# Chunk-selected attention followed by a gated feed-forward: constants in small parts, the first batch staged in half slots, a new order of work

## The chip, the cores and the metric

The kernel runs on one NeuronCore of a Trainium2 chip. The metric is device time in microseconds of one launch, measured over several runs; beside it stands one execution recorded by the hardware profiler. Engines are named as the profile names them: PE is TensorE's matmuls and PEld its weight loads, DVE is VectorE, ACT is ScalarE, POOL is GpSimd, and SP is SyncE, which in this kernel issues the DMAs. SPq is SyncE's queue.

## What is computed

Four batches of eight heads, 768 positions of 64 numbers each, in float32. The keys of a head are cut into 24 chunks of 32. For every query an upper bound of its product with any key of a chunk is formed from the chunk's smallest and largest key values, and only the six chunks with the highest bounds are attended to, causally. The result of all heads is the input of a feed-forward stage of width 2048 with a gate.

```python
k_min, k_max = np.min(k_chunks, axis=3), np.max(k_chunks, axis=3)
ub = np.sum(np.maximum(q * k_min, q * k_max), axis=-1)      # one bound for each query and chunk
ub = np.where(causal, ub, -1e9)
top_chunks = np.argsort(ub, axis=-1)[..., -6:]
scores = scale * np.matmul(q, k.transpose(0, 1, 3, 2))
scores = np.where(selected_chunk & (query_pos >= key_pos), scores, -1e9)
attn = softmax(scores)
x = np.matmul(attn, v)          # heads side by side: 3072 tokens x 512
h = x @ w_in                    # 512 -> 2048
g = h * np.clip(h + 3.0, 0.0, 6.0) / 6.0
out = g @ w_out                 # 2048 -> 512, float32
```

## The kernel before

**One list sets everything.** The work is cut into about 1,100 small steps. A text, `ORDER` (lines 34 to 108), lists them by short names; a loop at the end looks each name up in a table (line 620) and issues its instructions. Every engine works through its instructions in the order of that list, and so does SyncE through its DMAs; an instruction starts when its engine has come to it and what it reads or overwrites is ready or free. Nothing else orders the work: the place of a step in the list decides what stands before it on its engine. A letter at the end of a name (a, b, c, x, y) is the PSUM place that the step writes.

**Prologue.** `PRP` (line 259) lets GpSimd make the causal biases of the bounds (BIASM) and a chunk selector, built in a tile called E0 that lies inside XT; `PRI` (line 256) makes the identity that TensorE's transposes need, on GpSimd; `PRL` (line 273) casts the identity to bfloat16 and clears EM on VectorE; `PRD` (line 248) clears, on VectorE, a tiny tile, the operand of the warm-up matmuls (WARM, also inside XT) and constant columns of other tiles; `EG` (line 277) spreads the chunk selector into EM; `PRA` (line 245) runs one dummy exponential on ScalarE; `Z` (line 280) issues warm-up matmuls whose result is not used; `bd` (line 356), later, makes the biases of the other batches on GpSimd.

**Batch 0** is worked pair by pair: four pairs of heads, each in a first and a second half of 384 positions. `LK`, `LQ` and `LV` (line 363) load a half of one head's keys, queries or values, 98 KB each, from SyncE. `KT` and `QT` (line 375) turn a half, three 128x128 transposes on TensorE into PSUM. From there ScalarE casts it to bfloat16 (`KB`, `QB`), VectorE takes the largest and smallest key of each chunk (`MX`, `MN`, line 389), and the positive and negative parts of the queries are written (`RP` on ScalarE, `RN` on VectorE, `RA` on ScalarE; lines 399 to 409). `UH` forms the bounds on TensorE, `UB` adds the bias on VectorE, `TH` turns them, `T8` and `SE` find the six best chunks on VectorE, and `LH` and `MT` bring the choice back as a mask operand. `S` computes scores with the mask added in PSUM, `ex` exponentiates them on ScalarE (line 497), `af` cuts the causal triangle on GpSimd (line 501), `VC` casts a half of V on GpSimd (line 371), `A` and `B` multiply with V, and `na` and `nb` normalise on VectorE (line 534).

The inputs of batch 0 are staged in a float32 tile, STAGE, of six slots of 768 columns: K and Q of pairs 0 to 2 fill them, and pair 3 reuses those of pair 0 (lines 149 and 150). V has two slots (VS), pairs 0 and 2 in one, pairs 1 and 3 in the other.

**Batches 1 to 3** are worked four heads at once, a quad, of which there are two per batch, numbered 2 to 7. `lk` and `lq` load 192 KB for each head from SyncE into a third of STAGE (line 218), `lv` loads V for one pair; `kd` and `qd` are block transposes on VectorE (line 226), `mx` and `mn` reductions there (line 298), `kb` and `qb` casts on ScalarE, `rp` the positive part; `ud` forms the bounds, `us`, `tr`, `tm`, `se` and `tb` select on VectorE, and `mv` gathers on GpSimd; `SQ` computes scores for the quad.

**Feed-forward**: groups of 384 tokens, two per batch, numbered 0 to 7. `X` and `xe` turn the attention's result by TensorE for groups 0 to 2, `xt` (line 545) by DMA from SyncE for the rest. `wl` loads a quarter of a weight matrix, 1 MB (line 237), `wc` casts it on GpSimd (line 241): 0 to 3 are `w_in`, 4 to 7 `w_out`, through two buffers. A hidden step `H` is eight matmuls (line 562), with its gate on ScalarE (`hu`, line 571) and VectorE (`gt`, line 576). An output step `O` is four matmuls of 512 columns (line 597), four of them fill one PSUM bank, which `ot` unloads on ScalarE and `st` stores from SyncE.

## Time and profile before

| | |
|---|---|
| median of 3 runs | 284.9 us (283.8 to 286.69) |
| the profiled execution | 283.9 us, its span 282.2 us |
| PE busy | 261.6 us, 93% of the span |
| DVE busy | 182.9 us, 65% |
| ACT busy | 181.2 us, 64% |
| POOL busy | 104.6 us, 37% |
| read from HBM | 27.26 MB, written 6.29 MB |
| loads of batch 0's keys and queries | 32 of 96 KB, 2.4 and 2.5 us from issue to landing (medians) |

The span runs from the first to the last profiled instruction of the program; the profiled execution's own time contains it and 1.7 us around it. Busy time of PE comes from matmuls whose ends are modelled, so a busy PE is not a PE at its peak. A row of the timeline gives a start, a duration, engine, line of the kernel, operation, output and inputs and a count of merged instructions; behind it, in brackets, how long the engine stood idle before it and what ended that. A row of waits gives the waiting instruction, what it waited for, the total in microseconds, how often, and the longest.

### The profile page before, as it was taken

The page shows a single profiled execution, that of the slowest core. Times are in us where ns is not written, and L with a number is a line of the kernel's source. Part 1 is how long each engine was busy: PE and PEld are TensorE (multiplying, and loading weights), DVE is VectorE, ACT ScalarE, POOL GpSimd, SP SyncE. Part 2 cuts the span into 40 slices and gives each one's busy share as a digit, 9 for nine tenths or more (in the row PEclk, how much of TensorE's full clock was granted, in tenths as well). Part 3 has the DMA queues.
Part 4 walks back from the last instruction along what each step waited for, and adds up shares of the span by engine and source line. Part 5 has one row for each costly group of instructions (what it writes and reads, how often), then busy time and mean ns, then how long its engine had stood idle before and what let it go on. Part 6 is the DMA issues. An engine that isn't in the chain of part 4 may idle for free.

```text
span 282.2 us, 8568 instructions
## 1 busy us (share of the span) xinstructions
PE 261.6 (93%) x3549; PEld 153.7 (54%) x3549; DVE 182.9 (65%) x448; ACT 181.2 (64%) x251; POOL 104.6 (37%) x246
## 2 busy tenths in 40 slices
PE   0987998799999999999999999999999999999994
PEld 0555676566545456665555456665555555555561
DVE  1577798589997969999985538673783313622610
ACT  2377898347688648983567799878758752623621
POOL 6410296472860577540071454450481430000000
PEclk9999999999999999999999999999999999999999
DMA  5788449798999696494066544196000220221111
GB/s 128 162 192 178 163 96 324 155 324 251 247 242 205 173 202 151 92 222 65 2 144 132 126 92 110 41 200 118 6 0 14 103 56 2 74 95 38 74 55 58
DMA packets 91479, 36.08 MB, mean 128 GB/s; under 512 B 84144, under 2 KB 84400, under 8 KB 91440
## 3 DMA queue, kind: packets, MB, share of 16 engines
q1 hardware_dynamic: 91440, 35.53, 54.7%
q8 instruction: 28, 0.46, 0.7%
q14 instruction: 11, 0.09, 0.1%
HBM read 27.26 MB, written 6.29 MB: 119 GB/s over the span
## 4 chain that ended last, share of the span: by engine, by line
PE 63%; POOL 9%; DMA 8%; DVE 5%; issue 4%; ACT 3%; SPq 1%; POOLq 0%; DVEq 0%; ACTq 0%
PE PSx L604 12%; PE PSy L604 9%; PE PBa L566 8%; PE PBc L566 7%; PE PBb L566 7%; POOL MQ L353 4%; DMA WS<-in_moe_w_in_dram 3%; PE PSy L522 3%; DMA VS<-in_v_dram 2%; DMA STAGE<-in_q_dram 2%; PE PBb L604 2%; POOL WIN L243 2%; PE PBc L489 2%; PE PBb L489 2%; PE PBa L489 2%
## 5 line engine op out<-in xcount | busy, mean ns | idle before, releaser
L566 PEld LDWEIGHTS <-WIN 128*128 128x128 bf16 x512 | 49.0, 98 | 35.2 <-issue 1.5
L604 PEld LDWEIGHTS <-GT 128*128 128x128 bf16 x368 | 32.9, 98 | 38.9 <-issue 3.5
L506 POOL TENSOR_SCALAR_AFFINE_SELECT PT<-PT 128x256 bf16<-128x256 bf16 x78 | 30.4, 414 | 57.3 <-ACT PT L499 57.0
L604 PE MATMUL PSx<-WOUT,GT 128*128 128x512 bf16 x176 | 43.4, 380 | 0.6 <-POOL WOUT L243 0.6
L353 POOL COPY MQ<-MTM 32x144 bf16<-32x144 bf16 x96 | 29.4, 306 | 29.3 <-DVE MTM L347 25.0
L604 PE MATMUL PSy<-WOUT,GT 128*128 128x512 bf16 x144 | 35.1, 380 | 0.0
L499 ACT ACTIVATE PT<-PBc 128x1024 bf16<-128x1024 f32 (+2 forms) x29 | 25.7, 887 | 14.5 <-PE PBc L493 9.7
L566 PE MATMUL PBa<-XT,WIN 128*128 128x384 bf16 x184 | 33.7, 326 | 0.0
L574 ACT ACTIVATE U<-PBa 128x768 bf16<-128x768 f32 x23 | 18.7, 812 | 22.9 <-PE PBa L566 22.1
L566 PE MATMUL PBb<-XT,WIN 128*128 128x384 bf16 x160 | 29.3, 326 | 1.7 <-POOL WIN L243 1.3
L566 PE MATMUL PBc<-XT,WIN 128*128 128x384 bf16 x168 | 30.8, 326 | 0.0
L577 DVE SCALAR_TENSOR_TENSOR GT<-U,PBa 128x768 bf16<-128x768 bf16 x23 | 21.8, 947 | 13.1 <-ACT U L574 13.1
L577 DVE SCALAR_TENSOR_TENSOR GT<-U,PBc 128x768 bf16<-128x768 bf16 x21 | 20.0, 951 | 12.9 <-ACT U L574 12.8
L229 DVE STREAM_TRANSPOSE STAGE<-STAGE 128x768 f32<-128x768 f32 x24 | 23.0, 965 | 6.3 <-DMA STAGE<-in_q_dram 3.6
L499 ACT ACTIVATE PT<-PBb 128x1024 bf16<-128x1024 f32 (+2 forms) x25 | 23.5, 940 | 3.6 <-PE PBc L493 1.8
L574 ACT ACTIVATE U<-PBb 128x768 bf16<-128x768 f32 x20 | 16.2, 812 | 14.4 <-PE PBb L566 13.9
L499 ACT ACTIVATE PT<-PBa 128x1024 bf16<-128x1024 f32 (+2 forms) x24 | 22.7, 948 | 2.9 <-PE PBa L493 2.7
L577 DVE SCALAR_TENSOR_TENSOR GT<-U,PBb 128x768 bf16<-128x768 bf16 x20 | 19.0, 948 | 8.2 <-ACT U L574 7.9
L574 ACT ACTIVATE U<-PBc 128x768 bf16<-128x768 f32 x21 | 17.0, 810 | 9.4 <-PE PBc L566 8.4
L301 DVE TENSOR_REDUCE KMA<-STAGE 128x24 f32<-128x768 f32 x24 | 22.1, 940 | 0.1
L522 PEld LDWEIGHTS <-PT 128*128 128x128 bf16 x546 | 19.1, 97 | 3.9 <-issue 1.3
L489 PEld LDWEIGHTS <-KBA 32*128 32x128 bf16 x480 | 9.3, 92 | 16.5 <-issue 13.8
(191 smaller groups left out, 462.4 us busy)
## 6 DMA issues: line engine op xcount, KB each, us to landing
out_dram<-OT SPq DMA_DIRECT2D x23, 256.0 KB, 2.4
STAGE<-in_k_dram SPq DMA_DIRECT2D x24, 192.0 KB, 5.3
STAGE<-in_q_dram SPq DMA_DIRECT2D x24, 192.0 KB, 5.2
VS<-in_v_dram SPq DMA_DIRECT2D x12, 384.0 KB, 5.6
WS<-in_moe_w_in_dram SPq DMA_DIRECT2D x4, 1024.0 KB, 7.1
WS<-in_moe_w_out_dram SPq DMA_DIRECT2D x4, 1024.0 KB, 6.1
STAGE<-in_k_dram SPq DMA_DIRECT2D x16, 96.0 KB, 2.4
STAGE<-in_q_dram SPq DMA_DIRECT2D x16, 96.0 KB, 2.5
```

The source lines that it names most:

```text
L229: nc.vector.transpose(out=T, in_=T)
L243: nc.gpsimd.tensor_copy(WIN[:, :, 512 * c:512 * (c + 1)] if n < 4 else WOUT[:, 4 * c:4 * c + 4, :], WS[n % 2][:])
L301: nc.vector.tensor_reduce(out=dst, in_=staged("k", n)[:, h], axis=AX.X, op=(A.max, A.min)[w])
L353: nc.gpsimd.tensor_copy(MQ[n % 2][CH * g:CH * (g + 1), w * part:w * (part + 1)], MT4[n % 2][CH * part:CH * (part + 1), w * g:w * (g + 1)])
L489: nc.tensor.matmul(PSB[both[g // 2]][:, g % 2, at:at + w], lhsT=K[rows, x, j * P:(j + 1) * P], rhs=Q[rows, x, q0:q0 + w], start=(x == 0), ...
L499: nc.scalar.activation(pt(i, u)[:, :, 0:n], PSB[slot["S", i, u]][:, :, 0:n], ACT.Exp, scale=float(scale))
L506: nc.gpsimd.affine_select(out=T[:, :, lo:lo + P], in_=T[:, :, lo:lo + P], pattern=[[0, 2], [1, P]], compare_op=A.is_ge, fill=0.0, base=0, ...
L522: nc.tensor.matmul(O[:, e, t, :], lhsT=pt(i, u)[:, e, lo:lo + P], rhs=VB[i % 4][:, j, e, :], start=(j == 0), stop=(j == qb))
L566: nc.tensor.matmul(PSB[c][:, ff, 0:GRP], lhsT=WIN[:, kt, (2 * f + ff) * P:(2 * f + ff + 1) * P], rhs=XT[g % 3][:, kt, :], start=(kt == 0), ...
L574: nc.scalar.activation(slot["R", g, f][:], PSB[slot["H", g, f]][:, :, 0:GRP], ACT.Relu, bias=3.0)
L577: nc.vector.scalar_tensor_tensor(out=GT[g % 2][:, 2 * f:2 * f + 2, :], in0=slot["R", g, f][:], scalar=6.0, in1=PSB[slot["H", g, f]][:, :, ...
L604: nc.tensor.matmul(PSS[c], lhsT=GT[g % 2][:, f, t * P:(t + 1) * P], rhs=WOUT[:, f, :], start=(f == 0), stop=(f == FT - 1))
```

## The change

Three things are edited, and the list is written anew.

*Constants.* The five prologue steps become ten: `PW` clears the warm-up operand, `PT` the tiny tile, `PO` fills the constant columns, `PI` makes the identity, `PR` casts it, `PB` makes the biases of the bounds, `PF` fills E0 (on VectorE, before on GpSimd), `PC` cuts it on GpSimd, `PZ` clears EM and, new there, the bias tile of the other batches in one memset on VectorE, which `bd` cleared in four on GpSimd; `PA` is the dummy exponential. In the new list VectorE begins with `PW` and GpSimd with `PI`. There are six warm-up matmuls where there were five.

*Staging of batch 0.* STAGE is addressed by half slots: twelve of 384 columns, so that K and Q of all four pairs' first halves and of pairs 0 and 1's second halves have places of their own, and the second halves of pairs 2 and 3 reuse those of the first halves of pairs 0 and 1. V has one half slot for each pair; its second half follows into the same place after the first has been cast.

*Queues.* Six Q half loads (`AQ`: both heads of the first halves of pairs 0, 1 and 2) are issued from ScalarE's queue; three stand in the list ahead of the dummy exponential and three behind it. The other ten Q loads, all K and all V loads stay with SyncE.

*Order.* All other steps keep their instructions, with two exceptions in number: the negative part of second halves is written by VectorE for pairs 1 and 3 (`RN`) and by ScalarE for pairs 0 and 2 (`RA`), where ScalarE wrote all four. The first two lines of the new list, and pieces further on that the text below speaks of:

```diff
 ORDER = """
...
+PW AQ.2.0.1 LK.0.0.0 PT PI PO LK.0.1.1 AQ.0.0.1 PR Z.y.6 PZ PF PB LK.0.0.1 KT.0.0.b PC AQ.0.0.0 MX.0.0 EG.2 LK.1.0.1
+MN.0.0 EG.0 LK.1.0.0 PA EG.1 QT.0.0.y AQ.1.0.1 EG.3 AQ.1.0.0 LK.0.1.0 AQ.2.0.0 RP.0.0 RN.0.0 KT.1.0.a MN.1.0 MX.1.0
+KB.0.0 QB.0.0 QT.1.0.x KT.0.1.y RP.1.0 KB.1.0 RN.1.0 UH.0.0.c UH.1.0.b QB.1.0 MN.0.1 KB.0.1 LQ.0.1.1 UB.1.0 UB.0.0
...
+na.2 S.2.3.c ex.2.3 T8.3.1 LV.0.1.1 SE.3.1 wl.0 S.2.5.a X.0.1.x xe.0.1 S.2.2.b ex.2.2 LH.3.1.y MT.3.1 wc.0 af.0.2
+wl.1 kd.2.0 mx.2.0 H.0.1.c hu.0.1 ex.2.5 gt.0.1 mn.2.0 af.1.2 af.0.3 LV.0.1.0 VC.0.1 B.0.0.x H.0.0.b hu.0.0 gt.0.0
...
+qb.3.0 wl.6 wc.6 se.2.0 ud.3.b.a tb.2.0 mv.2.1 mv.2.0 us.3.1 tr.3.1 H.1.7.c hu.1.7 lv.5 wl.7 us.3.0 lk.4 H.1.4.a
+wc.7 hu.1.4 vc.5 gt.1.7 tm.3.1 O.0.2.2.x SQ.2.5.c.b lq.4 ex.5.5 gt.1.4 qb.3.1 O.0.0.2.y SQ.2.4.b.a ex.4.5 af.4.5
...
+gt.2.6 B.7.0.y qb.5.1 B.7.1.y B.6.1.x kb.5.1 nb.6 mv.4.1 SQ.4.4.b.c ex.9.4 H.2.7.a hu.2.7 nb.7 O.2.2.0.x lv.11 xt.3
+ex.8.4 gt.2.7 H.2.4.c hu.2.4 gt.2.4 SQ.4.5.a.b ex.9.5 tr.5.0 ex.8.5 tm.5.0 lk.7 tm.5.1 O.2.0.0.y O.2.0.1.y kb.5.0
+vc.8 SQ.4.0.a.c ex.8.0 se.5.0 tb.5.0 H.3.5.b ex.9.0 mv.5.0 hu.3.5 af.9.5 O.2.0.2.y O.2.0.3.y H.3.1.a af.8.5 gt.3.5
...
+hu.7.6 gt.7.6 H.7.7.a ot.6.1 hu.7.7 gt.7.7 H.7.2.b hu.7.2 gt.7.2 H.7.0.c hu.7.0 st.6.0 H.7.5.a hu.7.5 gt.7.0 H.7.4.b
+hu.7.4 gt.7.4 O.7.0.0.x O.7.0.1.x O.7.1.0.c O.7.1.1.c st.6.1 gt.7.5 O.7.0.2.x O.7.1.2.c O.7.1.3.c ot.7.1 O.7.0.3.x
...
-    KS = [STAGE[:, 2 * i % 6].rearrange("p (j e d) -> p j e d", e=2, d=D) for i in range(NPAIR)]
-    QS = [STAGE[:, (2 * i + 1) % 6].rearrange("p (j e d) -> p j e d", e=2, d=D) for i in range(NPAIR)]
+    FLAT = STAGE[:].rearrange("p a b -> p (a b)")
...
-    def prologue_dve():
+    def zero_warm():
+        nc.vector.memset(WARM, 0.0)
+
+    def zero_tiny():
         nc.vector.memset(TINY[:], 0.0)
-        nc.vector.memset(WARM, 0.0)
+
+    def fill_ones():
         for t in KM:
...
-    def prologue_ident():
+    def make_ident():
         make_identity(nc, IDENT32[:])
 
-    def prologue_pool():
+    def round_ident():
+        nc.vector.tensor_copy(IDENTB[:], IDENT32[:])
+
+    def bias_halves():
         nc.gpsimd.memset(BIASM[0:64], 0.0)
...
-        nc.gpsimd.memset(E0, E_VAL)
+
+    def fill_chunks():
+        nc.vector.memset(E0, E_VAL)
+
+    def cut_chunks():
         nc.gpsimd.affine_select(out=E0, in_=E0, pattern=[[P, NBLK], [1, P]], compare_op=A.is_ge,
...
-    def prologue_late():
-        nc.vector.tensor_copy(IDENTB[:], IDENT32[:])
+    def zero_masks():
         nc.vector.memset(EM[:], 0.0)
+        nc.vector.memset(BIAS4[:], 0.0)
...
             T = BIAS4[CH * g:CH * (g + 1)]
-            nc.gpsimd.memset(T, 0.0)
...
-    def half_load(x, kind, queue):
+    def half(m, i, h):
+        at = (8 * h + 2 * i + "KQ".index(m)) % 12 * SH
+        return FLAT[:, at:at + SH].rearrange("p (j e d) -> p j e d", e=2, d=D)
+
+    def half_load(x, m, queue):
         def issue(i, h, e):
             b, hp = divmod(i, NPAIR)
-            part = slice(3 * h, 3 * h + 3)
-            dst = VS[i % 2][:, e, part, :] if kind == "V" else (KS if kind == "K" else QS)[i][:, part, e, :]
-            queue.dma_start(dst, x[b, 2 * hp + e, SH * h:SH * (h + 1)].rearrange("(j p) d -> p j d", p=P))
+            queue.dma_start(half(m, i, h)[:, :, e, :], x[b, 2 * hp + e, SH * h:SH * (h + 1)].rearrange("(j p) d -> p j d", p=P))
+        return issue
+
+    def v_slot(i):
+        return VS[i // 2][:, :, 3 * (i % 2):3 * (i % 2) + 3, :]
+
+    def v_load(queue):
+        def issue(i, h, e):
+            b, hp = divmod(i, NPAIR)
+            queue.dma_start(v_slot(i)[:, e], v[b, 2 * hp + e, SH * h:SH * (h + 1)].rearrange("(j p) d -> p j d", p=P))
         return issue
 
     def v_half(i, h):
-        part = slice(3 * h, 3 * h + 3)
-        nc.gpsimd.tensor_copy(VB[i % 4][:, part, :, 0:D], VS[i % 2][:, :, part, :].rearrange("p e j d -> p j e d"))
+        nc.gpsimd.tensor_copy(VB[i % 4][:, 3 * h:3 * h + 3, :, 0:D], v_slot(i).rearrange("p e j d -> p j e d"))
```

The transposes and the readers of a turned half (`KT`, `QT`, `KB`, `QB`, `MX`, `MN`, `RP`, `RN`, `RA`) are rewritten to take the half slots, with the same instructions.

More of the change, by code (lines that the diff above doesn't have):

```diff
@@ L376, in issue, with half_transposes @@
+    def half_transposes(m):
         def issue(i, h, c):
-            slot[kind, i, h] = c
-            for t in range(3):
-                nc.tensor.transpose(PSS[c][:, t * P:(t + 1) * P],
-                                    ring[i][:, 3 * h + t].rearrange("p e d -> p (e d)"), IDENT32[:])
-        return issue
+            slot[m + "T", i, h] = c
+            for t in range(TPG):
+                nc.tensor.transpose(PSS[c][:, P * t:P * (t + 1)], half(m, i, h)[:, t].rearrange("p e d -> p (e d)"), IDENT32[:])
+        return issue
@@ L383, in k_half, with turned_half @@
+    def turned_half(m, i, h, first=0):
+        return PSS[slot[m + "T", i, h]][:, first:SH]
     def k_half(i, h):
-        nc.scalar.copy(KB[i % 4][:, SH * h:SH * (h + 1)], PSS[slot["KT", i, h]][:, 0:SH])
+        nc.scalar.copy(KB[i % 4][:, SH * h:SH * (h + 1)], turned_half("K", i, h))
     def q_half(i, h):
-        nc.scalar.copy(QB[i % 4][:, SH * h:SH * (h + 1)], PSS[slot["QT", i, h]][:, 0:SH])
+        nc.scalar.copy(QB[i % 4][:, SH * h:SH * (h + 1)], turned_half("Q", i, h))
     def reduce_half(m):
@@ L391, in issue @@
             nc.vector.tensor_reduce(out=KM[i % 4][:, m, 12 * h:12 * h + 12],
[L392 removed]
+                                    in_=turned_half("K", i, h).rearrange("p (c w) -> p c w", w=CH),
                                     axis=AX.X, op=(A.max, A.min)[m], negate=m == 1)
@@ L396, in part_of @@
     def part_of(R, i, h):
-        return R[i % 2][:, (0, Q0)[h]:(Q0, NQ)[h]], PSS[slot["QT", i, h]][:, (Q0, 0)[h]:SH]
+        return R[i % 2][:, (0, Q0)[h]:(Q0, NQ)[h]], turned_half("Q", i, h, (Q0, 0)[h])
     def plus_half(i, h):
```

143 lines of the change are left out of this document (65 added, 78 removed).

## The prediction

> **What bounds the kernel now.** I read the page first, then the busy time of the engines by stage, then the waits of TensorE, then the first 13 us instruction by instruction. The page's head and its first part:
>
> ```profile
> span 282.2 us, 8568 instructions
> PE 261.6 (93%) x3549; PEld 153.7 (54%) x3549; DVE 182.9 (65%) x448; ACT 181.2 (64%) x251; POOL 104.6 (37%) x246
> ```
>
> By stages (stretch, its length, busy us of PE, PEld, DVE, ACT and POOL with their instructions, granted clock, busy share of the DMA engines, GB/s):
>
> ```profile
> 0.00:30.00 30.00, 19.41 (x235) 12.55 (x237) 17.17 (x70) 16.43 (x35) 9.40 (x22) 1.00 0.75 170
> 30.00:60.00 30.00, 26.48 (x489) 19.64 (x491) 24.76 (x68) 22.63 (x28) 19.56 (x40) 1.00 0.74 203
> 60.00:100.00 40.00, 38.39 (x571) 20.58 (x566) 36.63 (x83) 28.22 (x39) 20.16 (x35) 1.00 1.01 229
> 100.00:145.00 45.00, 44.46 (x694) 26.47 (x676) 41.33 (x99) 31.02 (x43) 18.72 (x55) 1.00 0.61 114
> 145.00:235.00 90.00, 89.99 (x1354) 50.75 (x1353) 47.04 (x113) 65.45 (x84) 36.70 (x97) 1.00 0.40 87
> ```
>
> TensorE is idle 10.6 us in the first stage, 3.5 in the second, 1.6 in the third, 0.5 in the fourth and nothing in the fifth. So from about 60 us the matmuls are the limit, and what starts sooner there ends sooner. Before 60 us TensorE waits for others. In the third stage VectorE (36.6 of 40) and the DMA engines (share 1.01) are nearly as full as TensorE, which the rivals below rest on. TensorE's waits, longest first:
>
> ```profile
> PE PSy L282 <- DVE XT L250: 7.1, 1, 7.1
> PE PBb L566 <- POOL WIN L243: 1.3, 1, 1.3
> PE PBa L379 <- DVE MTM L454: 0.8, 1, 0.8
> ```
>
> One wait of 7.1 us at the very start is most of the first stage's idle time, and it is for a memset. The head in order of time (start, us, engine, line, operation):
>
> ```profile
> 0.81 1.28 ACT L246 ACT_TABLE_LOAD   x1 [0.81 <-PEq L655]
> 0.82 1.52 SPq L368 DMA_DIRECT2D STAGE<-in_k_dram  x3
> 2.58 0.73 POOL L267 MEMSET XT<- 32x768 bf16 x1
> 5.37 0.29 POOL masks.py:199 TENSOR_SCALAR_AFFINE_SELECT IDENT<-IDENT 128x128 f32<-128x128 f32 x1
> 5.70 0.23 DVE L274 CAST IDENTB<-IDENT 128x128 bf16<-128x128 f32 x1 [5.70 <-POOL IDENT masks.py:199]
> 6.77 0.27 DVE L250 MEMSET XT<- 128x256 uint32 x1
> 7.10 2.32 PE L282 MATMUL PSy<-XT 128*128 128x512 bf16 x5 [7.10 <-DVE XT L250]
> 9.21 0.85 PE L379 MATMUL PSy<-IDENT,STAGE 128*128 128x128 f32 x3
> 10.74 0.48 ACT L387 CAST QBA<-PBb 128x384 bf16<-128x384 f32 x1 [3.74 <-PE PBb L379]
> 12.89 0.55 PE L379 MATMUL PSy<-IDENT,STAGE 128*128 128x128 f32 x3
> 13.00 0.50 ACT L409 ACTIVATE WOUT<-PSx 128x384 f32<-128x384 f32 x1
> DMA to landing us min/median/max: 2.1/2.4/2.8
> ```
>
> The identity is made last on GpSimd (done at 5.7); VectorE's first instruction waits for it and stands ahead of the memset of the warm-up operand, so the warm-ups start at 7.10 and the first transposes of data at 9.21. Their data cannot be the reason: the third load is issued at 0.82 + 2 x 0.51 = 1.84 and lands, by the last row (of the loads issued in the first 12 us), 2.4 to 2.8 us later, at 4.2 to 4.6.
>
> **The change, step by step.**
>
> *Constants.* On GpSimd only the two identity instructions now precede everything; they are done near 0.8 + 0.5 = 1.3. VectorE's first instruction is the 0.27 us memset, so TensorE can begin at about 1.1. Six warm-ups instead of five at 0.43 (2.32 / 5, less the overlap of the last) end at 3.7. The first transposes then wait for data: 4.4 by the bound above, later if the loads that ScalarE issues beside them (three of 98 KB ahead of the first tile's last) take the engines; at the first stage's 170 GB/s the six loads issued by then, 0.59 MB, need 3.5 us from about 2, which ends at 5.4. I take 4.8. **Term 1: 4.8 - 9.2 = -4.4 us**, between -3.8 and -4.8. The memset of the chunk selector's source moves to VectorE (0.73 us on GpSimd; on VectorE not shown, between 0.07 and that) and the four bias memsets too, as one. VectorE has nothing to do before the first transposes end at 5.7, so they cost nothing; without that cover, at most 1 us.
>
> *ScalarE issues six loads.* The trace has no load from ScalarE; I price it as on SyncE, 0.51 each. Table load, six issues and the one dummy exponential end at 0.81 + 1.28 + 6 x 0.51 + 0.2 = 5.4. ScalarE's first data comes after the second transposes, near 6.5. Hidden by 1 us; if issues cost double there, two instructions of ScalarE wait 2 us, and the bounds of pairs 0 and 1 with them. Zero taken, bounds 0 and +2. SyncE's list of first loads gets 3.1 us shorter, but no row of TensorE's waits names a load, so that only gives room.
>
> *A half-rate TensorE.* The granted clock reads 1.00 throughout, yet three transposes took 0.85 at 9.21 and 0.55 at 12.89: TensorE ran slower for some 5 us after its first matmul. Before, four groups of three transposes fell into that (4 x 0.3 = 1.2 us). Now TensorE works 2.6 us, rests 1.1 and goes on with short pieces. If only the time since the first matmul counts, two groups are slow (-0.6); if the rest starts it anew, about eight are (+1.2). **Term 2: +0.4.**
>
> The Trainium skill (TensorE: Matmul & The Clock Gate, Part 1: The HAM clock gate) has the array at half rate until one window of about 3.4 us has been busy, and back to it after an idle one. Six warm-ups are shorter than that window, so by this rule the step costs the upper end, +1.2, and the forecast would be 0.8 higher. The trace agrees so far as it can: the slow stretch lasted about 5 us, between one window and two.
>
> *Positive and negative parts.* The order has two negative parts of a second half on VectorE that were on ScalarE. A 384-wide pass over PSUM on VectorE is not shown for this operation; the 192-wide one bounds it below and the reduction of the same 384 columns is the nearest row.
>
> ```profile
> 11.25 0.36 DVE L405 TENSOR_SCALAR WOUT<-PBb 128x192 f32<-128x192 f32 x1
> L391 DVE TENSOR_REDUCE KMA<-PSy 128x12 f32<-128x384 f32 x6 | 3.2, 553 | 3.2 <-PE PSy L379 2.5 <-ACT KBA L384 0.6
> ```
>
> Two at 0.55 are 1.1 us of VectorE (0.7 to 1.4), and ScalarE is rid of two at 0.50. VectorE is busy 83% in 30 to 60 us, a little less before, so I let half of it reach the end. **Term 3: +0.5**, between 0 and 1.4.
>
> *Slots of the first batch's inputs.* Keys and queries go half by half through twelve slots; four second halves reuse the slots of the first four tiles turned (free by about 8 us, when SyncE has got to them: 0.82 + 14 x 0.51 = 8.0). V has one half slot for each pair, where two pairs shared a whole slot. Before, that sharing shows here:
>
> ```profile
> 27.35 12.26 SPq L368 DMA_DIRECT2D VS<-in_v_dram  x5
> 51.47 0.51 POOL L373 CAST VB<-VS 128x384 bf16<-128x384 f32 x1 [4.01 <-DMA VS<-in_v_dram]
> 51.91 1.89 POOL L243 CAST WIN<-WS 128x2048 bf16<-128x2048 f32 x1
> 53.86 0.34 PE L566 MATMUL PBb<-XT,WIN 128*128 128x384 bf16 x1 [1.31 <-POOL WIN L243]
> ```
>
> Five issues that need 2.6 us took 12.3, since SyncE stood before a slot that GpSimd had not emptied, with weight loads queued behind. A V load then landed late, GpSimd waited 4.0 us for it, the weight cast behind it came late, and TensorE waited 1.31 (and 0.23 for the V cast). Now all four first halves load without a wait. In exchange, each second half waits for the cast of its own pair's first half, and SyncE's first two weight loads are queued behind the one of pair 0; that cast is ordered well ahead, so I price the new wait at nothing; without that cover the weights come as late as before. Of the 1.5 us I take most. **Term 4: -1.2**, between 0 and -2.5 (when more of the 3.5 us of idle time in this stage goes).
>
> *Two places of the new order with less cover.* Rows for them:
>
> ```profile
> 126.90 3.90 SPq L548 DMA_TRANSPOSE XT<-XB  x3
> DMA to landing us min/median/max: 2.4/2.5/4.0
> 208.22 1.30 PE PBb L566 x8
> 209.52 0.86 PE PSx L604 x4
> L574 ACT ACTIVATE U<-PBa 128x768 bf16<-128x768 f32 x23 | 18.7, 812 | 22.9 <-PE PBa L566 22.1
> L577 DVE SCALAR_TENSOR_TENSOR GT<-U,PBa 128x768 bf16<-128x768 bf16 x23 | 21.8, 947 | 13.1 <-ACT U L574 13.1
> L542 DVE TENSOR_TENSOR XB<-PSy,RINV 128x384 bf16<-128x384 f32 x13 | 7.2, 558 | 0.4
> ```
>
> For group 3 the activations are turned by DMA after pair 7's normalisation: 0.56 and more of it, a V load's issue of 0.5, and the last turn landing about 2.6 + 2.5 after the first issue, 6.2 us. TensorE has two hidden steps (1.30 each), three output steps (0.86) and three units of scores in between: 5.2 and those units. Exposed 0 to 1.5, taken 0.7. At the end, the gates of the last two hidden steps (0.81 + 2 x 0.95 = 2.7) face two output steps (1.7): 1.0 us, where one wait for a gate of 0.6 stands now; +0.4. **Term 5: +1.1.**
>
> **Sum:** -4.4 + 0.4 + 0.5 - 1.2 + 1.1 = -3.6 us. The profiled execution took 283.9 (span 282.2 and 1.7 around it), so 280.3; it lies 1.0 under the median 284.9 of the three runs (283.8 to 286.69), from which the same sum gives 281.3. **Forecast: 281.0 us.** About 1%, 2.85 us, is what a measurement of this kernel can tell from no change.
>
> **The rivals.**
>
> *VectorE takes the head's place* (283.5). For: 88% busy from 30 to 100 us. Ahead of the first bounds of batch 1 the new order has two more block transposes, three more reductions over a tile and one more gate, less one normalisation, against two more hidden steps on TensorE:
>
> ```profile
> L229 DVE STREAM_TRANSPOSE STAGE<-STAGE 128x768 f32<-128x768 f32 x24 | 23.0, 965 | 6.3 <-DMA STAGE<-in_q_dram 3.6 <-DMA STAGE<-in_k_dram 2.8
> L301 DVE TENSOR_REDUCE KMA<-STAGE 128x24 f32<-128x768 f32 x24 | 22.1, 940 | 0.1
> ```
>
> That is 1.9 + 2.8 + 0.9 - 0.7 = 4.9 us of VectorE for 2.6 of TensorE. If VectorE decides, 2.3 and the other half of term 3 are added: -3.6 + 2.3 + 0.6 = -0.7. Against: VectorE starts its data as much earlier as TensorE, and was 17% idle up to 60 us. The same time comes out if ScalarE's loads crowd the first tile and the head opens near 7 us: that the change doesn't do what it says.
>
> *The weights come late* (slower, 288.1). Place: the last weight cast.
>
> ```profile
> 81.26 1.89 POOL L243 CAST WOUT<-WS 128x2048 bf16<-128x2048 f32 x1 [1.94 <-DMA WS<-in_moe_w_out_dram]
> ```
>
> It already waits 1.94 us for its load. By the stages above some 16.1 MB had moved by 81.3 us (198 GB/s on the mean). The new order asks for the queries of the second quad and a V tile ahead of that cast, 17.4 MB against 16.25. At the old pace the extra 1.2 to 1.4 MB at 229 GB/s delay it 5.9 us; two output steps (1.7) are there to fill, and the end moves by 4.2 with the head's gain waiting in front of it. It decides if the mean pace stays below 17.4 / 81.3 = 214 GB/s; for the whole gain 17.4 / 76.9 = 226 is needed. Against: SyncE's stand of 9.7 us at 27 to 40 goes, which at 200 GB/s is worth 1.9 MB.
>
> *More than the head* (278). All 3.5 us of idle time in 30 to 60 goes, not 1.2: 281.0 - 2.3, and term 5 costs less.
>
> **How the numbers follow.** Forecast 0.45, VectorE or the crowded head 0.22, late weights 0.18, more than the head 0.15. Range 277.5 to 286: it leaves out the late weights and little else. Faster by over 1% (below 282.05): the best case and most of the forecast, 0.52. Within 1%: VectorE's case, the forecast's upper edge and a milder lateness, 0.30. Slower (above 287.75): 0.18.
>
> **What would show it.** First data transposes at 4.4 to 5.4 us (term 1), warm-ups from about 1.1; how many transpose groups take 0.85 (term 2); no stand of SyncE near 27 us and no TensorE wait for a weight cast (term 4); TensorE's idle time from 145 us on still near nothing, but a wait of group 3's first hidden step (term 5). The forecast is wrong if TensorE's idle time in 10 to 60 us grows by what the head gains, or if the last weight cast starts later than 81 us.

## The result and the profile after

The new kernel takes **276.9 us** (median of four, 275.69 to 277.94) where the kernel before took 285.8 beside it: a ratio of 0.969, with an interval of 0.962 to 0.977. Timed once more beside later runs it took 276.7 against 284.0, 0.975 (0.972 to 0.979). So the change gains 7 to 9 us. The forecast was 281.0 us, a gain of 3.9. Now and then an execution is 1 to 2% longer at a lower granted clock (one of four in the run with two small moves below, two of ten in that with the V slots), and the ratios and their intervals leave those out.

The profiled execution took 275.69, its span 274.0. First the page's head, then the same stretches of time as for the kernel before (stretch, its length, busy us of PE, PEld, DVE, ACT and POOL with their instructions, granted clock, DMA share, GB/s):

```profile
span 274.0 us, 8574 instructions
PE 261.3 (95%) x3550; PEld 153.7 (56%) x3550; DVE 184.0 (67%) x452; ACT 181.0 (66%) x249; POOL 102.6 (37%) x241
```

```profile
0.00:30.00 30.00, 25.36 (x360) 17.40 (x364) 24.43 (x103) 21.28 (x40) 13.67 (x34) 1.00 0.96 188
30.00:60.00 30.00, 26.91 (x484) 18.61 (x475) 27.38 (x53) 20.78 (x27) 17.42 (x25) 1.00 1.06 261
60.00:100.00 40.00, 40.00 (x650) 21.44 (x648) 35.31 (x103) 32.63 (x44) 26.40 (x61) 1.00 0.93 220
100.00:145.00 45.00, 45.00 (x615) 26.20 (x615) 35.00 (x68) 32.63 (x45) 17.32 (x46) 1.00 0.62 116
145.00:235.00 90.00, 89.31 (x1262) 51.11 (x1259) 50.47 (x117) 60.45 (x78) 27.78 (x76) 1.00 0.33 75
```

TensorE's busy time is the same (261.3 against 261.6), so the gain is idle time: 20.6 us of the span before, 12.7 after. It went in three places: 10.6 to 4.6 in the first stage, 3.5 to 3.1 in the second, and 2.1 to **nothing** in 60 to 145 us. 0.7 came back after 145. The DMA engines are now nearly full from the start to 60 us (shares 0.96 and 1.06), where they were at three quarters. Then the head, and behind it waits of TensorE that the text below reads (engine, tile and line, what it waits for; us in total, times, longest):

```profile
1.26 2.74 PE L292 MATMUL PSy<-XT 128*128 128x512 bf16 x6 [1.26 <-DVE TINY L251]
5.47 0.87 PE L398 MATMUL PBb<-IDENT,STAGE 128*128 128x128 f32 x3 [1.47 <-POOL XT L280]
6.14 0.85 PE L398 MATMUL PSy<-IDENT,STAGE 128*128 128x128 f32 x3
6.78 0.85 PE L398 MATMUL PBa<-IDENT,STAGE 128*128 128x128 f32 x3
7.95 0.87 PE L398 MATMUL PSx<-IDENT,STAGE 128*128 128x128 f32 x3 [0.33 <-DMA STAGE<-in_q_dram]
8.62 0.69 PE L398 MATMUL PSy<-IDENT,STAGE 128*128 128x128 f32 x3
10.03 0.55 PE L398 MATMUL PBa<-IDENT,STAGE 128*128 128x128 f32 x3
```

```profile
PE PBc L587 <- DVE GT L598: 1.4, 1, 1.4
PE PBa L587 <- DMA XT<-XB: 0.7, 1, 0.7
PE PBc L492 <- DVE GT L598: 0.7, 1, 0.7
PE PBc L625 <- DVE GT L598: 0.4, 2, 0.3
PE PBb L587 <- POOL WIN L242: 0.2, 1, 0.2
```

The warm-ups start at 1.26 and the first transposes of data at 5.47, after a rest of 1.47 us. The bracket names GpSimd's last cut in XT, which ends just then, but the transposes do not read XT: in a second profile of the same kernel the same wait, 1.63 us, is for the load of the keys. SyncE's stand ahead of a V slot has shrunk from 12.26 us for five issues to 3.06 for three. A new one, from 29.95 to 34.36, stands ahead of the third weight load, whose place the first weight cast on GpSimd empties at 34.33. What SyncE does where the first weights come, and the last weight cast:

```profile
25.81 1.04 SPq L238 DMA_DIRECT2D WS<-in_moe_w_in_dram  x2
26.89 3.06 SPq L388 DMA_DIRECT2D VS<-in_v_dram  x3
34.36 0.37 SPq L238 DMA_DIRECT2D WS<-in_moe_w_in_dram  x1
...
74.87 1.89 POOL L242 CAST WOUT<-WS 128x2048 bf16<-128x2048 f32 x1
```

The last weight cast starts at 74.87 instead of 81.26.

### The profile page after: what moved, and what is told of

It reads as the page before. It is cut to its first block, busy times and chain, and to the rows that moved or that the text cites. A ratio compares the mean times of both kernels' runs of the same rounds, so it can differ in the third digit from the quotient of the medians.

```text
span 274.0 us, 8574 instructions
## 1 busy us (share of the span) xinstructions
PE 261.3 (95%) x3550; PEld 153.7 (56%) x3550; DVE 184.0 (67%) x452; ACT 181.0 (66%) x249; POOL 102.6 (37%) x241
## 4 chain that ended last, share of the span: by engine, by line
PE 76%; DMA 13%; SPq 3%; DVE 3%; POOL 1%; ACT 1%; issue 1%; DVEq 0%
PE PSy L625 15%; PE PSx L625 10%; PE PBa L587 10%; PE PBc L587 9%; PE PBb L587 8%; DMA WS<-in_moe_w_in_dram 4%; DMA STAGE<-in_q_dram 4%; DMA STAGE<-in_k_dram 3%; PE PBa L510 3%; PE PSx L543 2%; PE PSy L543 2%; PE PBc L625 2%; PE PBc L510 2%; PE PBb L510 2%; PE PBb L333 2%; DMA XT<-XB 1%
## 5 line engine op out<-in xcount | busy, mean ns | idle before, releaser
L625 PE MATMUL PSy<-WOUT,GT 128*128 128x512 bf16 x192 | 46.8, 380 | 0.0
L587 PE MATMUL PBc<-XT,WIN 128*128 128x384 bf16 x184 | 33.7, 326 | 1.4 <-DVE GT L598 1.4
L598 DVE SCALAR_TENSOR_TENSOR GT<-U,PBa 128x768 bf16<-128x768 bf16 x22 | 20.9, 948 | 19.8 <-ACT U L595 19.8
L587 PE MATMUL PBa<-XT,WIN 128*128 128x384 bf16 x176 | 32.4, 326 | 1.3 <-DMA XT<-XB 0.7
L625 PE MATMUL PSx<-WOUT,GT 128*128 128x512 bf16 x128 | 31.8, 380 | 0.0
L598 DVE SCALAR_TENSOR_TENSOR GT<-U,PBc 128x768 bf16<-128x768 bf16 x23 | 21.8, 947 | 10.4 <-ACT U L595 10.3
L587 PE MATMUL PBb<-XT,WIN 128*128 128x384 bf16 x152 | 27.8, 326 | 0.2 <-POOL WIN L242 0.2
L595 ACT ACTIVATE U<-PBc 128x768 bf16<-128x768 f32 x23 | 18.7, 812 | 13.9 <-PE PBc L587 10.2
L520 ACT ACTIVATE PT<-PBc 128x1024 bf16<-128x1024 f32 (+2 forms) x26 | 24.2, 930 | 3.5 <-PE PBc L497 1.3
L520 ACT ACTIVATE PT<-PBa 128x1024 bf16<-128x1024 f32 (+2 forms) x26 | 23.9, 921 | 3.8 <-PE PBc L514 2.0
```

The lines of the kernel that those rows point to most:

```text
L520: nc.scalar.activation(pt(i, u)[:, :, 0:n], PSB[slot["S", i, u]][:, :, 0:n], ACT.Exp, scale=float(scale))
L587: nc.tensor.matmul(PSB[c][:, ff, 0:GRP], lhsT=WIN[:, kt, (2 * f + ff) * P:(2 * f + ff + 1) * P], rhs=XT[g % 3][:, kt, :], start=(kt == 0), ...
L595: nc.scalar.activation(slot["R", g, f][:], PSB[slot["H", g, f]][:, :, 0:GRP], ACT.Relu, bias=3.0)
L598: nc.vector.scalar_tensor_tensor(out=GT[g % 2][:, 2 * f:2 * f + 2, :], in0=slot["R", g, f][:], scalar=6.0, in1=PSB[slot["H", g, f]][:, :, ...
L625: nc.tensor.matmul(PSS[c], lhsT=GT[g % 2][:, f, t * P:(t + 1) * P], rhs=WOUT[:, f, :], start=(f == 0), stop=(f == FT - 1))
```

## The experiments

All times are medians. The kernel before took 284.0 to 284.7 us beside them (285.8 in the first comparison), and the new kernel 276.9 and 276.7, of which 276.8 is used; the medians of the kernel before lie up to 1.8 us apart between chips, so differences under 1 us are not read. Even a cost of 2 us that rests on medians of two chips is open in size: by the ratios, the intervals of the new kernel (0.962 to 0.977 and 0.972 to 0.979) overlap those of late constants, of one queue and of the cut at 57 us below, and not that of the three output steps put back. The theory at the start: the head carries to the end, and beyond it either the front (constants, queue, order of batch 0, slots) or the later order holds the part that the forecast missed. The rival: the DMA engines, now full to 60 us, hide what the head gains.

**One chip, four kernels: constants, and the order cut in two.** The eleven constant steps late in the new kernel:

```diff
-PW AQ.2.0.1 LK.0.0.0 PT PI PO LK.0.1.1 AQ.0.0.1 PR Z.y.6 PZ PF PB ... PC ... EG.2
+PT PB PF PC PI PR PZ EG.2 EG.1 PW PO Z.y.6 AQ.2.0.1 LK.0.0.0 LK.0.1.1 AQ.0.0.1 ...
```

> The new kernel with its eleven constant steps back in the old sequence (GpSimd's bias halves, chunk selector and identity first, VectorE's zeroing of the warm-up operand after them); loads and all else stay. First data transposes expected near 8.9 us, where the new kernel has 5.5. Theory A, the head reaches the end whole: 276.9 + 3.4 = 280.3 us, 279.5 to 281.2. Theory B, the first 58 us of the new kernel are set by the DMA engines (share 0.96 and 1.06 in its first two stages of 30 us), whose loads are issued when they were: the end moves by 0 to 1.2, 276.9 to 278.1.

Measured 278.8 (ratio 0.980, 0.974 to 0.986): +2.0, between the two theories. The first transposes start at 8.97. And the constants alone, early, in the kernel before:

```diff
-LK.0.0.1 PRP PRI PRL EG.2 EG.1 PRD Z.y.5 PRA EG.0 EG.3 LK.0.1.1 LK.0.0.0 KT.0.0.y
+PW LK.0.0.1 PT PI PO LK.0.1.1 PR Z.y.6 PZ PF PB LK.0.0.0 KT.0.0.y PC ...
```

> The kernel before with only the constants changed as in the new one: split into parts, zeroing of the warm-up operand and identity first, six warm-ups, chunk selector's and bias memsets on VectorE. Loads, slots and the order of everything else stay. First transposes of data at 4.4 to 5.4 us instead of 9.2. Theory A, the head reaches the end whole: 285.8 - 3.7 = 282.1 us, 281.3 to 282.9. Theory B, the waits of 10 to 60 us (VectorE 83% busy, loads) take its place: 284.5 to 286.

Measured 280.4 (0.984, 0.979 to 0.990): -4.4 beside its own 284.7. That is theory A and more: the head reaches the end whole in the old order. There the first transposes start at 4.59, in the new kernel at 5.47.

Now the order alone. The new order up to the sixth weight load (`wl.5`), then the old sequence:

```diff
 ... mv.2.3 lq.3 qd.3.0 qd.3.1 wl.5
-H.1.6.c kb.3.1 hu.1.6 gt.1.6 O.0.2.0.x tr.2.0 kx.3 H.1.5.a ... (new order)
+tr.2.0 O.0.1.0.x H.1.5.a hu.1.5 gt.1.5 qb.2.1 H.1.6.b hu.1.6 ... (what is left, in the old sequence)
```

> The new kernel with its order kept up to the sixth weight cast, about its first 57 us and 49 us of TensorE work, and what is left after that in the sequence of the order before. By TensorE's time less the work done so far, the new kernel leads by 6.0 us at that point (20.0 against 14.0) and by 8.3 at the end. Theory A, the lead is made in the front and the later order adds 2 to 3: 285.8 - 6.0 = 279.8 us, 279 to 281. Theory B, the front is all and the old remainder runs as well as the new one: 276.5 to 278. Theory C, the later order makes most of it: 281.5 or more.

Measured 279.7 (0.981, 0.975 to 0.988): theory A, 2.8 above the new kernel. So by the medians **about a third of the gain lies behind 57 us**. TensorE's waits of that run in 60 to 100 us:

```profile
PE PBa L586 <- DVE GT L597: 1.1, 1, 1.1
PE PSx L624 <- POOL WOUT L241: 0.6, 1, 0.6
PE PBa L586 <- DVE XT L579: 0.3, 1, 0.3
PE PBb L586 <- DVE GT L597: 0.2, 1, 0.2
```

Waits of the same two kinds, for a gate and for a weight cast, stand in the kernel before; in the new one there is none between 60 and 145 us:

```profile
73.48 1.46 PE L566 MATMUL PBb<-XT,WIN 128*128 128x384 bf16 x8 [0.37 <-DVE GT L577]
79.38 1.02 PE L604 MATMUL PSx<-WOUT,GT 128*128 128x512 bf16 x4 [0.64 <-POOL WOUT L243]
```

The other way about, the old front and the new remainder:

```diff
 ... us.2.0 tr.2.0 wl.4 us.2.1 tr.2.1 tm.2.1
-wc.4 O.0.1.0.x wl.3 H.1.5.a ... (old order)
+... lk.3 ... kd.3.1 ... wl.3 ... (what is left, in the new sequence)
```

> The other way about: the kernel before, with its constants, slots and order up to the fifth weight cast (about 62 us, 43 us of TensorE work), and what is left after that in the sequence of the new order. Theory A, the later order is worth 2 to 3 us by itself: 283 to 284. Theory B, the front is all: 285 to 286.5. Theory C, the later order makes most of the 8.9 us: 281.5 or less.

Measured 295.4 (1.037, 1.031 to 1.044): none of the three. The new remainder asks for quad 3's keys ahead of the fourth weight load, and the old front had not loaded them yet; TensorE then waited 8.2 us for GpSimd's weight cast:

```profile
69.97 2.74 PE L565 MATMUL PBb<-XT,WIN 128*128 128x384 bf16 x8 [8.16 <-POOL WIN L242]
```

The step behind the wait ran at half rate as well (2.74 us, where it takes 1.46 elsewhere; the last section has the clock). The cut made this wait, so the run tells nothing on the later order by itself. It does show how much a late weight can cost.

**Where behind 57 us, and the supply of loads.** The cut moved to 82 us:

```diff
 ... mv.3.2 mv.3.0 O.0.1.0.x
-O.0.1.1.x qd.4.1 SQ.2.3.b.a ... (new order)
+O.0.1.1.x O.0.1.2.x ... SQ.2.2.c.a ... (what is left, in the old sequence)
```

> The new order kept up to about 82 us (to quad 3's last selected rows and the first two output pieces behind them), the old sequence after that. With the cut at 57 us the gain was 3.4 us less than the new kernel's by the ratios, and TensorE was idle 2.1 us in 60 to 80 and 0.7 in 95 to 105 us, where the new kernel has none. Theory A, the new order's better part is 57 to 82 us, where the w_out weights, the gates and quad 3's selection meet: 277 to 278 us. Theory B, it lies later, at the selections of quads 4 and up: 279 to 280.

Measured 276.6 (0.973, 0.967 to 0.979), the new kernel's time within 1 us and a little under the range of theory A: the better stretch is 57 to 82 us. The difference there that can be seen in the order: the new one sets output steps of group 0 between the last hidden steps of group 1, where the old one has five and more hidden steps in a row. Moved back, alone:

```diff
-H.1.6.c kb.3.1 hu.1.6 gt.1.6 O.0.2.0.x tr.2.0 ... H.1.0.c rp.3.0 O.0.0.1.y gt.1.2 ... gt.1.0 O.0.2.1.x qb.3.0 ... O.0.2.2.x
+H.1.6.c kb.3.1 hu.1.6 gt.1.6 tr.2.0 ... H.1.0.c rp.3.0 gt.1.2 ... gt.1.0 qb.3.0 ... O.0.2.0.x O.0.0.1.y O.0.2.1.x O.0.2.2.x
```

> The new kernel with one thing of the old order: the first three of group 0's output steps that stand between the late hidden steps of group 1 (at 64 to 72 us) are moved behind them, so that five hidden steps follow each other, as in the order before. Nothing else moves. With the old sequence from 57 us on, TensorE waited there 1.12 and 0.24 us for gates (the activation of 0.81 on ScalarE and the product of 0.95 on VectorE, against 1.30 of TensorE, on a VectorE that is full) and 0.64 us for a weight cast. Theory A, this interleaving is the later order's gain: 276.9 + 2.0 = 278.9 us (278 to 279.7). Theory B, the gain lies in the earlier keys and queries of quad 3 or elsewhere: 276.3 to 277.4.

Measured 279.8 (0.987, 0.980 to 0.994): +3.0, theory A, and a little more than its range. TensorE's steps of this run between 61 and 84 us that it had to wait for (start, busy us, what, in brackets the idle time before it and its releaser):

```profile
68.22 1.46 PE L586 MATMUL PBc<-XT,WIN 128*128 128x384 bf16 x8 [0.78 <-DVE GT L597]
70.97 0.31 PE L332 MATMUL PBb<-RPA,KMA 32*32 32x144 f32 x2 [1.29 <-DVE GT L597]
```

2.1 us of waits for gates, where the new kernel has none. VectorE is the engine behind both. It is full in 60 to 70 us in this run (9.97 of 10 us) and in the new kernel (10.00, the third number of the row), whose TensorE is full all the same:

```profile
60.00:70.00 10.00, 10.00 (x68) 5.31 (x74) 10.00 (x29) 8.15 (x12) 5.22 (x10) 1.00 0.83 253
```

A hidden step takes TensorE 1.30 us and VectorE 0.95 for its product, beside the selections of quads 2 and 3; an output step takes TensorE 0.86 and VectorE nothing. So by these rows each output step set in between gives VectorE 0.86 us to catch up.

Two tries to better the supply, since SyncE issues nothing from 29.95 to 34.36:

```diff
-LV.1.1.0 VC.1.1 ... wl.2 wc.2 B.1.0.y B.1.1.y nb.1 lk.3 ... wl.3 ... lq.2
+LV.1.1.0 VC.1.1 ... lk.3 wl.2 wc.2 B.1.0.y B.1.1.y nb.1 ... wl.3 ... lq.2   (first try)
+LV.1.1.0 VC.1.1 ... lk.3 wl.2 wc.2 B.1.0.y B.1.1.y nb.1 ... lq.2 wl.3 ...   (second try)
```

> The new kernel with one load moved: the keys of quad 3 (four issues of SyncE) stand ahead of the third weight load instead of behind it. SyncE has nothing to issue from 29.95 to 34.36 us, since that weight load waits for a slot that GpSimd's first weight cast empties; the keys' own slot is free by then. Theory A, the supply of loads sets 42 to 58 us of the new kernel: the keys land some 4 us earlier, VectorE's wait of 1.27 us for them at 44.5 goes, the queries of quad 2 behind them come about 2 us earlier, and of TensorE's idle time of 3.1 us in 30 to 60 us about half goes: 276.9 - 1.5 = 275.4 us (274.5 to 276.2). Theory B, the DMA engines are full anyway (share 1.06): what the keys gain the weights lose, 276.5 to 278.

> As the run with the keys of quad 3 ahead of the third weight load, and the queries of quad 2 ahead of the fourth weight load as well. Theory A: VectorE's wait for the queries (0.47 us at 52.4) goes too, but the fourth weight load lands 2 us later and GpSimd's fourth weight cast, at 47.1, with it: 274.5 to 276. Theory B: that cast holds TensorE's seventh hidden step: 277 to 279.

Measured 279.3 (0.981) and 280.5 (0.986), +2.5 and +3.7: theory A is out in both, and the loss is larger than the range of theory B. In the first try SyncE's issue of the keys took 6.9 us instead of 4.8, and the third weight load went out at 36.2 instead of 34.4. TensorE waited for weights, 1.4 us in the first try and 2.9 in the second:

```profile
PE PBc L586 <- POOL WIN L241: 2.9, 1, 2.9
```

The trace shows the loss for the second try alone. In the first, the wait of 1.4 us only replaces one of 1.45 that the new kernel has for a gate two hidden steps later, at 47.37; its profiled execution, 277.1 us and the shortest of four, does not show the loss of the median. The stand leaves little to gain: the DMA engines are full in most of it (share 1.05 and 1.10 in 30 to 34 us, 0.51 in the two behind), so a load that goes ahead there delays another.

**The V slots.** In the kernel before, with the slot of each pair and a sequence of V loads to suit:

```diff
-LV.0.1.1 ... LV.0.0.1 ... LV.0.1.0 ... LV.0.0.0 ... LV.1.0.1 VC.0.0 ... LV.1.0.0 VC.1.0 ... LV.1.1.1 ... VC.0.1 B.0.0.y wl.0
+LV.0.0.1 ... LV.0.0.0 ... LV.1.0.1 ... LV.1.0.0 ... LV.3.0.0 VC.0.0 ... wl.0 LV.0.1.1 VC.1.0 ... LV.0.1.0 ... VC.0.1 B.0.0.y
```

> The kernel before with one half slot of V for each pair, as in the new kernel; the V loads take the same places of the order in a sequence that suits it (first halves of all pairs ahead), and the first weight load stands ahead of the first V load that now waits. Constants, keys, queries and the rest stay. Theory A, as predicted for term 4: SyncE's stand of 9.7 us near 27 goes, the weights come earlier and 1.2 us of TensorE's idle time go (0 to 2.5): 285.2 - 1.2 = 284.0 us, 282.7 to 284.8. Theory B, the slots by themselves move nothing that TensorE waits for: 284.8 to 286.

Measured 284.9 against 284.3, a ratio of 1.0007 (0.997 to 1.004): theory B, nothing. But the edit did not do what the expectation said: SyncE still stands, now ahead of the second half of pair 0, whose slot GpSimd's cast empties at 35.8 in the old order:

```profile
25.43 0.49 SPq L238 DMA_DIRECT2D WS<-in_moe_w_in_dram  x1
35.86 4.71 SPq L376 DMA_DIRECT2D VS<-in_v_dram  x7
```

In the new kernel the V casts start at 24.7 us instead of 35.3, since its order of batch 0 asks for them sooner. So the slots alone do not end the stand. That the earlier casts do it is read from these times; no run has the new order with the old slots.

**The second queue.** All of the new kernel's loads on SyncE:

```diff
-PW AQ.2.0.1 LK.0.0.0 ... AQ.0.0.1 ... AQ.0.0.0 ... AQ.1.0.1 EG.3 AQ.1.0.0 LK.0.1.0 AQ.2.0.0
+PW LQ.2.0.1 LK.0.0.0 ... LQ.0.0.1 ... LQ.0.0.0 ... LQ.1.0.1 EG.3 LQ.1.0.0 LK.0.1.0 LQ.2.0.0
```

> The new kernel with the six query loads of batch 0 that ScalarE issues put on SyncE's queue, in the same places of the order. SyncE then has twenty-two loads at 0.5 us each instead of sixteen in the first part, and the last of the first two pairs' data is issued about 3 us later. Theory A, TensorE meets those loads with 1 us or less to spare, as it waits 0.33 us for a query tile at 7.9 already: 276.9 + 1 to 3 = 278 to 280 us. Theory B, the queue is no matter: 276.3 to 277.5.

Measured 278.4 (0.981, 0.974 to 0.988): +1.6, theory A. What DMA moved in the first 12 us, in the new kernel (with the row of ScalarE's queue, the share is that of 16 engines) and in this run:

```profile
DMA packets 8953, 2.20 MB, mean 184 GB/s; under 512 B 8953, under 2 KB 8953, under 8 KB 8953
q10 hardware_dynamic: 2400, 0.59, 26.4%
```

```profile
DMA packets 7301, 1.80 MB, mean 150 GB/s; under 512 B 7301, under 2 KB 7301, under 8 KB 7301
```

One queue at half a microsecond for each load of 96 KB leaves the engines a third idle (share 0.66 in these 12 us); with ScalarE's six loads they are full (1.02), 0.4 MB further on after 12 us, and the first weight load goes out at 25.8 instead of 28.5. The first transposes start no sooner with one queue (5.63), since the query loads then stand ahead of the first keys on SyncE. The same in the kernel before, beside early constants:

```diff
-LK.0.0.0 KT.0.0.y LQ.0.0.0 MX.0.0 MN.0.0 LQ.0.0.1 QT.0.0.b QB.0.0 LQ.0.1.1 ... LQ.0.1.0 ... LQ.1.1.0 ... LQ.1.1.1
+PW AQ.0.0.0 LK.0.0.1 PT PI PO AQ.0.0.1 ... LK.0.0.0 KT.0.0.y AQ.0.1.1 PC AQ.0.1.0 MX.0.0 ... PA AQ.1.1.0 EG.1 AQ.1.1.1 QT.0.0.b
```

> The kernel before with the constants as in the new one and the first six query loads (both halves of pair 0, the second half of pair 1) issued from ScalarE, as far ahead as in the new kernel; the order of the rest stays. The run with the constants alone took 280.4 us. Theory A, the second queue is worth 1.5 to 3 us whatever the order: 277.4 to 279. Theory B, it pays only with the new sequence of batch 0, which takes the first halves of two pairs at once and so asks for the data faster: 279.8 to 281.

Measured 280.5 (0.987, 0.982 to 0.992), as without the queue: theory B. The first transposes start at 5.59 here and at 4.59 in the run with the constants alone, so ScalarE's loads do crowd the first tile, by 1.0 us. Whether the old order cannot use the data sooner, or wins back later just what the first tile loses, the times do not tell.

**All three undone.** What is still open then is whether constants, queue and interleaving add up. The three edits above (late constants, every AQ an LQ, the three output steps behind) in one kernel:

> The new kernel with three parts undone at once: the constants in the old sequence, all loads from SyncE, and the three output steps of group 0 behind the hidden steps of group 1. What is left of the change is the half slots, the V slots and the rest of the new order. Alone the three cost 3.0, 3.2 and 5.0 us by the ratios (1.9, 1.5 and 2.9 by the medians). Theory A, they add up and hold the whole gain: 283.2 to 288, about the 284.5 of the kernel before. Theory B, they share one slack and overlap: 279.5 to 282.5, and the rest of the change is worth 2 to 5 us.

Measured 280.9 (0.989, 0.985 to 0.992): theory B. One by one the three cost 2.0, 1.6 and 3.0 by the medians, 6.6 in sum; together 4.2 (280.9 against 276.7 on that chip). The traces show which of them overlap. The first hidden step, in the new kernel (two profiles), with late constants, with one queue and with all three undone:

```profile
34.97 1.47 PE L587 MATMUL PBc<-XT,WIN 128*128 128x384 bf16 x8
35.24 1.47 PE L587 MATMUL PBc<-XT,WIN 128*128 128x384 bf16 x8
38.01 1.47 PE L586 MATMUL PBc<-XT,WIN 128*128 128x384 bf16 x8
36.91 1.47 PE L586 MATMUL PBc<-XT,WIN 128*128 128x384 bf16 x8
38.00 1.47 PE L586 MATMUL PBc<-XT,WIN 128*128 128x384 bf16 x8
```

By here late constants cost about 2.9 us, one queue about 1.8, and both together no more than late constants alone. So with a late head one queue is enough. The waits for gates of the three output steps come on top, 0.78 and 1.29 us with all three undone as with the output steps alone. The remaining 3.0 us below the kernel before belong to what is left, the half slots and the rest of the new order; no run parts these. With the head as late as before (first transposes at 8.97) TensorE is idle 8.8 and 3.1 us in the first two stages, against 10.6 and 3.5.

```profile
0.00:30.00 30.00, 21.20 (x299) 14.39 (x301) 21.47 (x96) 18.16 (x35) 11.87 (x29) 1.00 0.74 162
30.00:60.00 30.00, 26.89 (x476) 19.13 (x477) 28.75 (x54) 23.81 (x31) 17.82 (x29) 1.00 1.08 267
```

**The half rate, and a better version.** Nine warm-ups instead of six:

```diff
-PR Z.y.6 PZ PF PB
+PR Z.y.9 PZ PF PB
```

> The new kernel with nine warm-ups instead of six, so that TensorE works from 1.26 to about 5.2 us without the rest of 1.47 us ahead of the first data transposes. Theory A, the half rate ends after a stretch of unbroken work: it ended 4.8 us after the first matmul in the kernel before and 3.2 us after it in the run with late constants, which both went from the warm-ups straight into the data, and only 7.5 us after it in the new kernel, which rested. Then it ends here between 4.5 and 6.1 us, three to four groups of transposes take 0.55 instead of 0.86, and the end moves by 0 to -1.2: 275.7 to 276.9 us. Theory B, the rest has nothing to do with it: the groups stay slow to about 8.7 us, 276.9 to 277.3. The Trainium skill (TensorE: Matmul & The Clock Gate, Part 1: The HAM clock gate) lets a free-running window of about 3.4 us that is busy end the half rate; by it nine warm-ups reach the point and six do not.

Measured 275.5 (0.970, 0.963 to 0.978), -1.3 by the medians, and by the ratios between nothing and -1.4 us. The mechanism is theory A: TensorE no longer rests, the third group is at full rate, and the first hidden step starts at 34.48, 0.5 and 0.8 us before the two profiles of the new kernel:

```profile
1.26 4.02 PE L291 MATMUL PSy<-XT 128*128 128x512 bf16 x9 [1.26 <-DVE TINY L250]
5.42 0.88 PE L397 MATMUL PBb<-IDENT,STAGE 128*128 128x128 f32 x3
6.09 0.76 PE L397 MATMUL PSy<-IDENT,STAGE 128*128 128x128 f32 x3
6.69 0.49 PE L397 MATMUL PBa<-IDENT,STAGE 128*128 128x128 f32 x3
```

With two small moves more:

```diff
-Z.y.6 ... SQ.6.5.c.b ex.13.5 af.13.5 H.5.6.a ex.12.5 O.4.2.2.y hu.5.6 ... ot.7.0 st.7.1 O.7.2.0.b ... ot.7.2 st.7.2 st.7.0
+Z.y.9 ... SQ.6.5.c.b ex.13.5 af.13.5 O.4.2.2.y H.5.6.a ex.12.5 hu.5.6 ... ot.7.0 st.7.0 st.7.1 O.7.2.0.b ... ot.7.2 st.7.2
```

> The new kernel with three small changes: nine warm-ups instead of six; the third piece of group 4's last output step ahead of group 5's first hidden step, which waits 0.7 us there for the activations turned by DMA; and the output step that is written as two halves of 256 columns made the one that really ends the kernel, so that the last eviction is 0.39 us instead of 0.60 and the last store half as large. Theory A: -0.7 - 0.5 - 0.3 from 276.9 gives 275.4 us (274.6 to 276.2). Theory B, what the first two give is lost in later waits: 276.3 to 277.3.

Measured 275.0 (0.967, 0.960 to 0.974). The gap to the new kernel was too small to read across chips, so both were timed on one:

> The new kernel unchanged, beside the version with nine warm-ups and the two small moves on the same chip: 276.4 to 277.4 us, and the beginning of the full clock again at another time than in the first profile if it falls by chance.

> The version with nine warm-ups, the covered wait of group 5 and the split last output step, timed beside the new kernel on the same chip. Theory A, it is 1 to 1.5 us shorter: 275 to 276. Theory B, no difference that can be measured: 276.3 to 277.3.

276.7 (0.975, 0.972 to 0.979) and **274.3** (0.965, 0.963 to 0.968): theory A and somewhat more, 2.4 us better than the new kernel, with intervals that do not touch. The wait of group 5 for its turned activations (0.9 in the run beside it) is gone, and the last eviction unloads half an output tile, 0.38 us instead of 0.60. How the 2.4 us divide among the three edits was not measured:

```profile
267.20 1.91 PE L612 MATMUL PBc<-WOUT,GT 128*128 128x256 bf16 x16
...
269.15 0.38 ACT L614 ACTIVATE OT<-PBc 128x256 f32<-128x256 f32 x1 [1.36 <-PE PBc L612]
```

## Why the prediction was wrong, step by step

**The step that failed is term 5, the last of the sum, and with it the way the sum was made.** Term 5 went through the new order looking for places with less cover, found two and added 1.1 us; it did not look for places with more. The gates and the w_out casts of 57 to 82 us were such a place: output steps set between hidden steps are worth 2.8 to 3.0 us there by two runs, 2.1 of it seen as waits, a loss priced where a gain stood. The idle time was in the table of stages, 1.6 and 0.5 us in the third and fourth; the argument read "from about 60 us the matmuls are the limit" and gave that time no term. The second miss is the step on ScalarE's issues, taken as 0, below.

**The head** (-4.4): the transposes moved by 3.74, just under the stated bound of 3.8; they start at 5.47, where the working with crowded loads had 5.4. The crowding is shown in the old order alone (4.59 to 5.59). There the head by itself was worth 4.4 us at the end. In the new order it is worth 2.0 by the medians and 2.9 at the first hidden step.

**The half rate** (+0.4): four and a half slow groups against four before in this execution, about +0.1. In other executions of the same front five and six groups were slow. The sign was right: with the rest the half rate lasts longer than without.

**ScalarE's issues** (0): three took 1.60 us and two 1.33, and ScalarE's first data came later. But the step treated a shorter SyncE list as mere room, since no TensorE wait named a load. Undone, it cost 1.6 by the medians and 1.8 at the first hidden step: with the new order and an early head TensorE takes the data faster than one queue brings it. That is a gain without a term, tied to the order of batch 0, for which there was no term either.

**Negative parts on VectorE** (+0.5): not tried by itself. VectorE is busier (27.4 of 30 us in the second stage) and TensorE's idle time there is no larger, so nothing speaks for a cost.

**V slots** (-1.2): the stand ahead of a V slot shrank, but the slots alone did nothing; in the new order the V casts come 10.6 us earlier. What the shorter stand is worth was not isolated. TensorE's wait for a w_in cast is 0.2 us now, where it was 1.31.

**Less cover** (+1.1): no wait at group 3, where 0.7 was priced, but 0.7 at group 5 for the same kind of turn: the size is luck, the place was wrong. At the last gates 1.0 us was priced in place of 0.6; measured are 0.4, so the end got better by 0.2 and not worse by 0.4.

**The rivals.** VectorE as the bound did not come: 35.3 of 40 us busy in the third stage, and TensorE without a pause; with the three output steps moved back, TensorE waits for VectorE. The late weights did not come either. The condition in the prediction was a pace of 226 GB/s for the whole gain, and the trace shows 233 up to the last cast:

```profile
0.00:74.87 74.87, 67.14 (x1036) 44.60 (x1037) 65.69 (x190) 51.59 (x79) 39.67 (x76) 1.00 1.00 233
```

(Up to its own last cast the kernel before had moved 206 GB/s, 16.7 MB, not the 16.1 that the prediction took from the stages.) The first weights have little to spare too: with keys and queries loaded ahead of them TensorE waited 2.9 us for a w_in cast. "More than the head" had the sign, at 278 and with a chance of 0.15, and the wrong place: of the 3.5 us of idle time in 30 to 60 only 0.4 went, so its coming nearest is luck.

## What to carry to other kernels

Where an order written by hand is replaced, price it in both directions: go through the stretches in which another engine is full, and ask what TensorE work without need of that engine stands there before and after. Idle time of a per cent or two in a stage that looks full (38.4 of 40) is still worth a term when the whole change is worth three per cent. Parts of a change can need each other, and can hide each other: the second queue was worth 1.6 to 1.8 us with the new order and an early head, and nothing in the old order or with a late head. So a part undone alone tells what it is worth beside the others, not what it would bring by itself.
